# One maximum shared by two heads in pairs 3 to 10 of an attention and feed-forward kernel

## The chip, the cores and the metric

The kernel runs on one core of a Trainium2 chip. The metric is the device time of one launch in microseconds (us). Before the change it is 1376.97 us, the median of three runs (1376.26 to 1377.02).

## What is computed

Attention over 8 batches, 12 heads, 448 tokens and a head size of 64, with normalised q and k, and then a feed-forward layer over the 3584 tokens (768 wide, 2048 inside). Cut to what matters:

```
q_n, k_n = rmsnorm(q, g_q), rmsnorm(k, g_k)
scores = scale * (q_n @ k_n^T)
scores = scores - max(scores)            # per query
attn = exp(scores);  attn = attn / (sum(attn) + 1e-9)
x = (attn @ v), heads side by side       # 3584 x 768
r = relu(x @ w_in);  out = (s * r * r + b) @ w_out
```

The inputs are float32, and q, k, v and both gains come eight times as large as usual, so that scores are far apart. The kernel keeps the products exact by splitting a number into a high part in the format float32r, which TensorE multiplies in one pass, and the rest in a second one.

## The kernel before

Heads go in pairs: 48 pairs p = 0 to 47, six for each batch. A pair has eight slots, and slot 8p + 4j + kc holds one score tile `st` of head j: 128 keys against all 448 queries. One loop over slots writes every engine's instructions, and each engine runs its own in that order; PE is TensorE, DVE VectorE, ACT ScalarE, POOL GpSimd, and SP issues all DMA transfers, each once the semaphores of what it reads have come. What goes into a slot is set by `at(slot, function, ...)` and, for the maxima, by the table `scores`.

For a pair whose first slot is s0 = 8p, the steps near the change are, for p = 3 to 10:

- `load_rows` brings rows of k and q, `norm_rows` normalises them, `turn` transposes them on TensorE into `tk`, and `split_turned` (p under 8) or `split_both` and `split_lows` (from 8 on) write `ka` and `qa`. `ka` holds k's high part in rows 0 to 63 and its low part in rows 64 to 127; `qa` holds q's high part twice. For the second head this is at slots s0-9 and s0-8.
- `score` multiplies high and low k with every fourth query's high part, 112 queries by 448 keys, into the PSUM tile `sh`, and `maximum` takes the largest per query on DVE into a column of `nmx`. There are eight of them in a pair, c = 0 to 3 for the first head and 4 to 7 for the second, one to a slot, ten slots ahead of the slot with the same number: c = 3 in slot s0-7, c = 4 in s0-6, c = 7 in s0-3.
- `shift` moves the four columns of a head with a DMA into a row of `qb` (L431, `qb<-nmx`), in slots s0-6 and s0-2; `double_kb` copies k's high part into `kb` (`kb<-ka`).
- `score_t` (L496 and L499) writes the score tile with the shift already subtracted, ACT takes the exponential, and `weigh` multiplies it with v (`av`).
- `take`, `gather`, `invert` and `divide` bring the sums of the exponentials through DRAM: row to column (`zt`), inverse on DVE, out to `z_d`, and back as `zb`, spread over 64 rows for each head, in slot s0+16 of a pair. Slot s0-8 of one pair is slot s0+16 of the pair three before, and SP's order there is that of the pairs, the older first (pair 5's `zb` is entered by a loop of its own and stands behind).

From pair 12 (`TURNED`) on, a pair takes seven maxima: six over 128 of the first 384 queries, each third one, and one over the last 64 queries of both heads at once, which multiplies `qz` (the two heads' queries on the diagonal, zeros elsewhere) with `kh`, the high parts of both heads' k one above the other. There ACT writes both (`split_kq`, `both_k`). From pair 7 on, TensorE also runs the first feed-forward product of the batch before (`ph`), and DVE, ACT and POOL turn the weights, which come as 64-bit words (`w64i`), into two float32r parts (`wai`, `wih`, `wil`) in the first twelve pairs.

Of the kernel before, what the change touches and what calls it, by code (L numbers as in the profile page):

```python
# [9 lines left out]
F32 = mybir.dt.float32  # L10
F32R = mybir.dt.float32r
I32 = mybir.dt.int32
AF = mybir.ActivationFunctionType
ALU = mybir.AluOpType
# [11 lines left out]
AHEAD = 10  # L26
# [11 lines left out]
SHIFTED = {0: -9, 1: -8, 2: -7, 3: -6, 4: -4, 5: -3, 6: -2, 7: -1, 8: 1, 9: 1, 10: 2, 11: 2, 12: 4, 13: 4, 14: 5, 15: 5, 16: 8, 17: 8, 18: 9, 19: 10}  # L38
# [9 lines left out]
TURNED = 12  # L48

APART = 8  # L50

PLAIN = 11

THIRD = (11, 14, 17)

# [6 lines left out]
def attention_then_relu2_ffn(  # L62
# [30 lines left out]
    V, S, G, T = nc.vector, nc.scalar, nc.gpsimd, nc.tensor  # L93

    NPAIR, P, _, SEQ = kq.shape
# [4 lines left out]
    D = P // 2  # L100
    NP = NPAIR // B
    H = 2 * NP
    TILES = 2 * SEQ // P
    NV = PLAIN
    NQ = 4
    QC = SEQ // NQ
    WHOLE = SEQ // P * P
# [3 lines left out]
    NKC = 4  # L111
# [6 lines left out]
    W = 8  # L118
# [22 lines left out]
    def psum(name):  # L141

        bank = free.pop(0)
        return ps.tile([P, 512], F32, tag=bank, name=name), bank
# [85 lines left out]
    with tc.tile_pool(name="apool", bufs=1) as ap:  # L230
        khs = {}
        raws, kqs, invs, vrs, nmxs, shs, tks = ({} for _ in range(7))
# [102 lines left out]
        vs = [None, None]  # L335
# [10 lines left out]
        def split_v(p):  # L346
            n = p % 2
            if vs[n] is None:
                vs[n] = ap.tile([P, NKC, 2, 3, D], F32R, tag=f"vs{n}", name=f"vs{n}")
                for m in range(2):  # L350
                    G.memset(vs[n][:, :, m, 1].bitcast(F32), 1.0 - m)
            vr, to = vrs.pop(p), vs[n]
            S.copy(to[:, :, 0, 0:3:2], vr)
            G.tensor_tensor(to[:, :, 1, 0:3:2], vr, to[:, :, 0, 0:3:2].bitcast(F32), ALU.subtract)  # L354

        def norm(p):

# [38 lines left out]
        ka = [ap.tile([P, 2 * SEQ], F32R, name=f"ka{n}") for n in range(2)]  # L396
        qa = [ap.tile([P, 2 * SEQ], F32R, name=f"qa{n}") for n in range(2)]
        kb = [ap.tile([P, 2 * SEQ], F32R, name=f"kb{n}") for n in range(2)]
        qb = [ap.tile([P, 2 * SEQ], F32R, name=f"qb{n}") for n in range(2)]
        qz = ap.tile([P, P], F32R, name="qz")  # L400
        G.memset(qz.bitcast(F32), 0.0)
        for t in qb:
            G.memset(t[D:P].bitcast(F32), 0.0)
        vfs = [ap.tile([P, NKC, 3, D], F32, tag=f"vs{n}", name=f"vf{n}") for n in range(2)]
        for t in vfs:
            G.memset(t[:, :, 1], 1.0)
            G.memset(t[:REST, 3, 1], 0.0)
# [3 lines left out]
        def split_kq(p, j):  # L411

            t, n = kqs[p, j], p % 2
            a = slice(j * SEQ, (j + 1) * SEQ)
            S.copy(ka[n][:, a], t[:, 0])  # L415
            S.copy(qa[n][:, a], t[:, 1])
            half = slice(j * D, (j + 1) * D)
            S.copy(qz[half, half], t[half, 1, WHOLE:])
            yield
            G.tensor_tensor(ka[n][D:, a], t[D:, 0], ka[n][D:, a].bitcast(F32), ALU.subtract)  # L420
            G.tensor_tensor(qb[n][:D, a], t[:D, 1], qa[n][:D, a].bitcast(F32), ALU.subtract)  # L421

        def both_k(p):
            kqs.pop((p, 0))
# [5 lines left out]
        def move(to, of):  # L430
            nc.sync.dma_start(to.bitcast(F32), of.bitcast(F32))  # L431
# [5 lines left out]
        def score(i):  # L437

            p, c = divmod(i, W)
            j, c = divmod(c, NQ)  # L440
            sh, bank = psum(f"sh{i}")
            a = slice(j * SEQ, (j + 1) * SEQ)
            shs[i] = sh, bank
            if p >= TURNED:
                q, k = qz, khs.get(p)
                if i % W != 3:
                    q = qa[p % 2][:, a][:, :WHOLE].rearrange("k (p c) -> k c p", c=3)[:, c]
                    k = ka[p % 2][:, a]
                else:
                    khs.pop(p)  # L450
                T.matmul(sh[:, :SEQ], q, k, start=True, stop=True)  # L451
                return
            T.matmul(  # L453
                sh[:QC, :SEQ], qa[p % 2][:, a].rearrange("k (p c) -> k c p", c=NQ)[:, c],
                ka[p % 2][:, a], start=True, stop=True,
            )

        def maximum(i):
            p, c = divmod(i, W)
            if c == 0:  # L460
                nmxs[p] = bounds.tile([P, W], F32R, tag="nmx", bufs=2, name=f"nmx{p}")
            sh, bank = shs.pop(i)
            n = QC if p < TURNED else P
            V.tensor_reduce(  # L464
                out=nmxs[p][:n, c : c + 1], in_=sh[:n, :SEQ], op=ALU.max, axis=AX.X, negate=True
            )
            free.append(bank)

        def shift(p, part):

            to = qb[p % 2][D : D + 1, part * SEQ : (part + 1) * SEQ]
            if p < TURNED:
                of = nmxs[p][:QC, part * NQ : (part + 1) * NQ]
                move(to.rearrange("o (p c) -> o p c", c=NQ), of)
            else:
                of = nmxs[p][:, 4 * part : 4 * part + 3]
                move(to[:, :WHOLE].rearrange("o (p c) -> o p c", c=3), of)
                of = nmxs[p][part * D : (part + 1) * D, 3:4]
                move(to[:, WHOLE:].rearrange("o (p c) -> o p c", c=1), of)
            if part:  # L480
                nmxs.pop(p)
# [59 lines left out]
        def weigh(i):  # L541


            p, j, kc, rows = chunk(i)
            if kc == 0:
                avs[p, j] = psum(f"av{p}_{j}")
            av = avs[p, j][0]
            moved = movers.pop(i)
            if p < NV:
                of = vrs[p].rearrange("p c u d -> p c (u d)")  # L550
                todo = [(of[:, kc, j * D : j * D + P], moved[0])]
            else:
                of = vs[p % 2].rearrange("p c m u d -> p c m (u d)")
                hi, lo = (of[:, kc, m, j * D : j * D + P] for m in range(2))
                todo = [(hi, moved[0]), (lo, moved[0])] + [(hi, a) for a in moved[1:]]
            for m, (x, a) in enumerate(todo):
                T.matmul(  # L557
                    av[:, :SEQ], x, a,
                    start=kc == 0 and m == 0, stop=kc == 3 and m == len(todo) - 1,
                )  # L560
# [141 lines left out]
        def at(s_, f, *a):  # L702
            jobs[s_].append((f, a))
# [4 lines left out]
        for p in range(NPAIR):  # L708
            s0 = W * p
            if p >= TURNED:  # L710
                late_by = 2 if p == TURNED else 0
                at(s0 - 32 + 2 * late_by, load, p)
                after_x = 1 if p % NP == NP - 1 else 0
                at(s0 - 28 + late_by + after_x, norm, p)
                at(s0 - 24 + late_by + after_x, keep, p)
            for j in range(2):
                s1 = s0 + 4 * j
                steps = SOONER.get((p, j), (s1 - 20, s1 - 14, s1 - 13, s1 - 10, s1 - 6))
                if p >= TURNED:
                    apart = 1 if p % NP == 3 and j == 0 else 0  # L720
                    at(s1 - 19 + apart, load_kq, p, j)
                    at(s1 - 19 + (apart if j == 0 else 1), spread, p, j)
                    at(s1 - 15 + apart, scale, p, j)
                    at(s1 - 15 + apart, multiply_q if apart else scale_q, p, j)
                    at(s1 - 13, split_kq, p, j)
                    if j:
                        at(s0 - 8, both_k, p)
                else:
                    at(max(s1 - 28, FIRST), load_rows, p, j)
                    if s1 == 0:  # L730
                        at(FIRST, gains)
                    at(steps[0], norm_rows, p, j)
                    at(steps[1], turn, p, j)
                    if p < APART:
                        at(steps[2], split_turned, p, j)
                    else:
                        at(steps[2], split_both, p, j)
                        at(steps[2] + 1, split_lows, p, j)
                at(steps[3], double_kb, p, j)
                at(steps[4], shift, p, j)  # L740
                at(s1 + 6, take, p, j)
                at(s1 + 7, gather, p, j)
            at(s0 - (9 if p >= NV else 5), load_v, p)
            if p >= NV:
                at(s0 - 3, split_v, p)
            at(s0 + 13, invert, p)
            for step in (1, 2, 3):
                if p % NP < NP - 1:
                    at(s0 + 12 + 2 * step, divide, p, step)
# [21 lines left out]

        scores = {}
        for i in range(NSLOT):
            if i // W >= TURNED and i % W == W - 1:
                continue
            scores.setdefault(SHIFTED.get(i, i - AHEAD), []).append(i)

        def within(i):
            return 0 <= i < NSLOT
# [2 lines left out]
        with tc.manual_schedule(engines=ORDERED):  # L782
            begun = []
            for s_ in range(FIRST, NSLOT + START + NCC):
# [34 lines left out]
                b, m = divmod(s_ + 1 - START, W * NP)  # L819
# [271 lines left out]
```

## Time and profile before

| | before |
|---|---|
| median of three runs | 1376.97 us |
| span of the profiled execution, first to last instruction | 1375.6 us |
| busy PE, DVE, ACT, POOL | 99%, 77%, 68%, 44% of the span |
| maxima on DVE (L464) | 348 instructions, 212.8 us |
| score matmuls for them (L451, L453) | 252 + 96 by the maxima's shapes |

The span runs from the first to the last instruction of one profiled execution, and the median of the timed runs is 1.4 us above it. A share is busy time over the whole span. PE's records overlap, because matmuls are pipelined and their ends are modelled, so a matmul's own duration is longer than the distance from one start to the next. In the rows below SPq is SP's DMA queue, and its durations are those of the issue, not of the transfer.

### The profile page before, as it was taken

The numbers are of one execution on the slowest core, as the hardware profiler recorded it, in microseconds if no ns is written. First come the engines' busy times: TensorE is split into PE (matmuls) and PEld (weight loads), VectorE is DVE, ScalarE is ACT, GpSimd is POOL, SyncE is SP. The second block draws the span as 40 slices with busy tenths as digits, with TensorE's granted clock in tenths as the row PEclk, the third lists the DMA queues.
The fourth block names the chain that finished last, engine by engine and source line by source line (L and its number), as shares of the span: only waits on it lengthen the run. The fifth ranks groups of instructions, "written<-read, shape, count | busy, mean of one in ns | idle before, by whom it ended". The sixth has DMA issues, their size and how long they took to land.

```text
span 1375.6 us, 21578 instructions
## 1 busy us (share of the span) xinstructions
PE 1363.6 (99%) x6970; PEld 1255.6 (91%) x6970; DVE 1057.3 (77%) x1572; ACT 937.2 (68%) x1727; POOL 603.1 (44%) x486
## 2 busy tenths in 40 slices
PE   8999999999999999999999999999999999999998
PEld 7767789999999999999999999999999999999998
DVE  7999997897888798688788878526766676666763
ACT  6886778888888888888888887636544434344431
POOL 6875787766667666676667665100000000000000
PEclk9999999999999999999999999999999999999999
DMA  4555676787788788778778867356543332343330
GB/s 133 150 145 169 181 232 197 230 249 214 223 235 239 222 243 232 221 222 250 229 220 240 236 204 211 104 197 222 186 119 118 88 91 90 95 121 112 85 90 35
DMA packets 262800, 243.39 MB, mean 177 GB/s; under 512 B 85280, under 2 KB 244000, under 8 KB 262688
## 3 DMA queue, kind: packets, MB, share of 16 engines
q1 hardware_dynamic: 262688, 242.03, 60.0%
q8 instruction: 55, 0.90, 0.3%
q14 instruction: 57, 0.47, 0.1%
HBM read 177.21 MB, written 53.38 MB: 168 GB/s over the span
## 4 chain that ended last, share of the span: by engine, by line
PE 92%; DVE 4%; ACT 2%; DMA 1%; issue 1%; SPq 0%; POOL 0%; DVEq 0%; POOLq 0%; ACTq 0%
PE ph L198 32%; PE p L936 30%; PE av L557 15%; PE st L496 5%; PE st L499 5%; PE sh L451 4%; PE sh L453 1%; DVE nmx L464 1%; PE tk L282 1%; DVE wai L154 1%; DVE ssq L260 0%; DVE wai L152 0%; DVE wai L157 0%; DMA zb<-z_d 0%; ACT e L511 0%
## 5 line engine op out<-in xcount | busy, mean ns | idle before, releaser
L198 PE MATMUL ph<-x,wih 128*128 128x448 f32 x1536 | 488.3, 365 | 0.0
L198 PEld LDWEIGHTS ph<-x,wih 128*128 128x128 f32 x1536 | 289.0, 188 | 28.7 <-issue 6.1
L198 PE MATMUL ph<-x,wil 128*128 128x448 f32 x768 | 293.3, 382 | 0.0
L515 ACT ACTIVATE st<-st 128x448 f32<-128x448 f32 (+1 forms) x296 | 155.9, 527 | 104.1 <-PE st L499 102.7
L464 DVE TENSOR_REDUCE nmx<-sh 128x1 fp32r<-128x448 f32 (+1 forms) x348 | 212.8, 616 | 12.0 <-PE sh L451 6.3
L538 DVE TENSOR_TENSOR low<-st,ah 128x448 fp32r<-128x448 f32 x222 | 136.7, 616 | 47.2 <-ACT ah L523 42.5
L557 PE MATMUL av<-ah,vs 128*128 128x448 f32 x592 | 168.7, 366 | 0.0
L496 PE MATMUL st<-qa,ka 128*128 128x448 f32 (+1 forms) x384 | 159.1, 414 | 2.3 <-DVE nmx L464 2.2
L198 PEld LDWEIGHTS ph<-x,wil 128*128 128x128 f32 x768 | 144.3, 188 | 17.0 <-issue 6.2
L523 ACT CAST ah<-st 128x448 fp32r<-128x448 f32 (+1 forms) x296 | 156.9, 530 | 2.0
L499 PE MATMUL st<-qb,kb 128*128 128x448 f32 (+1 forms) x384 | 140.3, 365 | 0.0
L557 PEld LDWEIGHTS av<-ah,vs 128*128 128x128 f32 x592 | 111.2, 188 | 8.6
L921 ACT CAST hi<-a 128x1024 fp32r<-128x1024 f32 x54 | 56.8, 1053 | 91.0 <-PE p L936 74.0
L420 POOL TENSOR_TENSOR ka<-kq,ka 64x448 fp32r<-64x448 f32 x72 | 86.2, 1198 | 56.3 <-ACT ka L415 53.0
L603 POOL TENSOR_TENSOR u<-uz,zb 128x448 f32<-128x448 f32 x48 | 59.9, 1247 | 95.9 <-DMA zb<-z_d 75.9
L421 POOL TENSOR_TENSOR qb<-kq,qa 64x448 fp32r<-64x448 f32 x72 | 95.3, 1323 | 5.4
L369 POOL TENSOR_TENSOR ri<-ri,mhalf 128x14 f32<-128x14 f32 x36 | 93.6, 2601 | 3.0
L922 DVE TENSOR_TENSOR lo<-s,hi 128x1024 fp32r<-128x1024 f32 x41 | 50.1, 1222 | 52.1 <-ACT hi L921 52.1
L218 ACT ACTIVATE r<-ph 128x448 f32<-128x448 f32 x128 | 69.7, 545 | 27.6 <-PE ph L198 15.8
L354 POOL TENSOR_TENSOR vs<-vr,vs 128x512 fp32r<-128x512 f32 x37 | 49.4, 1336 | 86.0 <-DMA w64o<-in_dram 31.4
L496 PEld LDWEIGHTS st<-qa,ka 128*128 128x128 f32 (+1 forms) x384 | 68.2, 178 | 20.2 <-DVE nmx L464 6.1
L385 POOL TENSOR_TENSOR kq<-kq,rb 128x448 f32<-128x448 f32 x72 | 86.5, 1202 | 0.0
(253 smaller groups left out, 3256.4 us busy)
## 6 DMA issues: line engine op xcount, KB each, us to landing
kq<-in_dram SPq DMA_DIRECT2D x72, 448.0 KB, 5.1
rb<-i_d SPq DMA_DIRECT2D x72, 448.0 KB, 4.8
r_d<-r SPq DMA_DIRECT2D x128, 224.0 KB, 3.7
a<-r_d SPq DMA_DIRECT2D x48, 512.0 KB, 4.9
raw<-in_dram SPq DMA_DIRECT2D x36, 448.0 KB, 5.0
w64i<-in_dram SPq DMA_DIRECT2D x24, 512.0 KB, 4.5
w64o<-in_dram SPq DMA_DIRECT2D x48, 256.0 KB, 4.1
kb<-ka SPq DMA_DIRECT2D x96, 112.0 KB, 2.8
```

Of the source, the lines that this page charges most:

```text
L198: T.matmul(ph[:, :SEQ], w[:, cc, f0 : f0 + P], xs[b, cc][:, part, :], start=cc == 0 and m == 0, stop=cc == NCC - 1 and m == 2,)
L369: G.tensor_tensor(ri, ri, mhalf[:, :n], ALU.pow)
L385: G.tensor_tensor(t[:, 0], t[:, 0], rb[:, 0], ALU.mult)
L421: G.tensor_tensor(qb[n][:D, a], t[:D, 1], qa[n][:D, a].bitcast(F32), ALU.subtract)
L464: V.tensor_reduce(out=nmxs[p][:n, c : c + 1], in_=sh[:n, :SEQ], op=ALU.max, axis=AX.X, negate=True)
L496: T.matmul(st[:rows, :SEQ], ka[n][:, keys], qa[n][:, q], start=True, stop=False)
L499: T.matmul(st[:rows, :SEQ], kb[n][:, keys], qb[n][:, q], start=False, stop=True,)
L515: S.activation(st[:rows, :SEQ], st[:rows, :SEQ], AF.Exp)
L523: S.copy(ah[:rows], sts[i][0][:rows, :SEQ])
L538: V.tensor_tensor(al, st[:rows, :SEQ], ah[:rows].bitcast(F32), ALU.subtract)
L557: T.matmul(av[:, :SEQ], x, a, start=kc == 0 and m == 0, stop=kc == 3 and m == len(todo) - 1,)
L936: T.matmul(po, a[:, f], w[:, f], start=f == 0 and m == 0, stop=f == NH - 1 and m == 2,)
```

## The change

Pairs 3 to 10 take seven maxima too. `score` and `maximum` go the way of the later pairs for them. `last_queries` lets ACT copy the last 64 queries of each head into `qz`, and `join_k` lets two DMAs move the high parts of both heads' k from `ka` into `kh`; both are entered in slot s0-8. The shared maximum, c = 3, goes from slot s0-7 to s0-6, where c = 4 is, and c = 7 falls away. The shift of the first head goes one slot later, to s0-5, and each shift takes two DMAs instead of one. `kh` lies in the room of v's low part, which these pairs don't use yet; for that the tile `vs` is cut into two. Lines of the changed kernel are up to 21 higher: L467 and L469 are the score matmuls, L447 the moves, L598 `zt`, L614 `zb`.

```
+SHARED = frozenset(range(3, PLAIN))
...
-                vs[n] = ap.tile([P, NKC, 2, 3, D], F32R, tag=f"vs{n}", name=f"vs{n}")
+                vs[n] = [ap.tile([P, NKC, 3, D], F32R, tag=f"v{x}{n}", name=f"v{x}{n}") for x in "hl"]
...
+        def shared(p):
+            return p >= TURNED or p in SHARED
+
+        def last_queries(p):
+            for j in range(2):
+                half = slice(j * D, (j + 1) * D)
+                S.copy(qz[half, half], qa[p % 2][half, j * SEQ + WHOLE : (j + 1) * SEQ].bitcast(F32))
+
+        def join_k(p):
+            kh = khs[p] = ap.tile([P, SEQ], F32R, tag=f"vl{p % 2}", name=f"kh{p}")
+            for j in range(2):
+                a = slice(j * SEQ, (j + 1) * SEQ)
+                move(kh[j * D : (j + 1) * D], ka[p % 2][:D, a])
...
-            if p >= TURNED:
+            if shared(p):
                 q, k = qz, khs.get(p)
...
-            n = QC if p < TURNED else P
+            n = P if shared(p) else QC
...
-            if p < TURNED:
+            if not shared(p):
                 of = nmxs[p][:QC, part * NQ : (part + 1) * NQ]
...
-                at(steps[4], shift, p, j)
+                at(steps[4] + (p in SHARED and j == 0), shift, p, j)
+                if p in SHARED and j:
+                    at(steps[3] - 2, last_queries, p)
+                    at(steps[3] - 2, join_k, p)
...
-            if i // W >= TURNED and i % W == W - 1:
+            if shared(i // W) and i % W == W - 1:
                 continue
-            scores.setdefault(SHIFTED.get(i, i - AHEAD), []).append(i)
+            sooner = AHEAD - (i // W in SHARED and i % W == NQ - 1)
+            scores.setdefault(SHIFTED.get(i, i - sooner), []).append(i)
```

On SP the first place is pair 3's slots 16 to 19. Before, with `zb_700` of pair 0, row loads of pairs 5 and 6, and the moves of pair 3 (`kb_194`, `qb_196`):

```order
L597 DMA zb_700<-z_d_87 64x448 x2
L245 DMA rows_1_705<-in_dram 112x512
L431 DMA qb_196<-nmx_672 1x112x4
L431 DMA kb_194<-ka_190 64x448
L581 DMA zt_656<-zr_735 64x1x7
```

and now:

```order
L614 DMA zb_700<-z_d_87 64x448 x2
L447 DMA kh_705<-ka_190 64x448 x2
L247 DMA rows_1_710<-in_dram 112x512
L447 DMA kb_194<-ka_190 64x448
L598 DMA zt_656<-zr_737 64x1x7
L447 DMA qb_196<-nmx_672 1x128x3
L447 DMA qb_196<-nmx_672 1x64x1
```

The two joining moves stand behind `zb`, and the shift, now in two pieces, stands behind the doubling of `kb` and the gathering of `zt`.

On PE the place is pair 3's slots 16 to 18, `sh` being the maxima's score tiles (c = 2, 3 and 4 of pair 3 before) and `tk` the transposes of pair 4:

```order
L453 MATMUL sh_707<-ka_190,qa_192 112x448
L557 MATMUL av_1_675<-e_648,vf_202 128x448
L496 MATMUL st_712<-qa_191,ka_189 128x448
L499 MATMUL st_712<-qb_195,kb_193 128x448
L453 MATMUL sh_719<-ka_190,qa_192 112x448
L557 MATMUL av_1_675<-e_680,vf_202 128x448
L496 MATMUL st_724<-qa_191,ka_189 128x448
L499 MATMUL st_724<-qb_195,kb_193 128x448
L282 MATMUL tk_0_0_740<-ident,rows_0_460 64x112 x4
L282 MATMUL tk_0_1_745<-ident,rows_0_460 64x112 x4
L453 MATMUL sh_750<-ka_190,qa_192 112x448
```

and now:

```order
L467 MATMUL sh_712<-ka_190,qa_192 128x448
L574 MATMUL av_1_675<-e_648,vf_202 128x448
L512 MATMUL st_717<-qa_191,ka_189 128x448
L515 MATMUL st_717<-qb_195,kb_193 128x448
L574 MATMUL av_1_675<-e_680,vf_202 128x448
L512 MATMUL st_726<-qa_191,ka_189 128x448
L515 MATMUL st_726<-qb_195,kb_193 128x448
L284 MATMUL tk_0_0_741<-ident,rows_0_460 64x112 x4
L284 MATMUL tk_0_1_746<-ident,rows_0_460 64x112 x4
L467 MATMUL sh_751<-kh_705,qz 128x448
L467 MATMUL sh_753<-ka_190,qa_192 128x448
```

The slot in the middle has no score matmul any more, and the one that reads `kh` and `qz` stands right ahead of c = 4, behind the transposes.

## Rows read from the trace of the kernel before

**Rows 1.** Three stretches: length, busy us (instructions) of each engine, granted clock, DMA.

```profile
core 0: us, PE busy (x) PEld busy (x) DVE busy (x) ACT busy (x) POOL busy (x), PEclk, DMA share, GB/s
...
28.00:68.00 40.00, 39.87 (x175) 28.73 (x174) 36.97 (x70) 35.07 (x70) 27.71 (x24) 1.00 0.55 150
68.00:139.00 71.00, 67.25 (x286) 49.28 (x284) 68.37 (x111) 56.17 (x109) 46.84 (x38) 1.00 0.56 157
139.00:175.00 36.00, 35.74 (x159) 29.26 (x160) 34.01 (x53) 27.50 (x51) 28.75 (x21) 1.00 0.63 180
```

**Rows 2.** PE's waits from 68 to 139 us: total us, times, longest us.

```profile
PE st L496 <- DVE nmx L464: 1.6, 2, 0.8
PE sh L453 <- DVE nmx L464: 1.1, 1, 1.1
PE sh L453 <- DVE ka L310: 0.6, 1, 0.6
```

**Rows 3.** Instructions by line and form: busy us, mean ns of one, idle before.

```profile
L464 DVE TENSOR_REDUCE nmx<-sh 112x1 fp32r<-112x448 f32 x96 | 57.5, 614 | 2.1 <-PE sh L453 1.7
...
L453 PE MATMUL sh<-ka,qa 128*112 128x448 f32 x96 | 38.5, 418 | 3.5 <-DVE ka L294 1.2 <-DVE nmx L464 1.1 <-DVE ka L310 0.6
```

**Rows 4.** Line 418, ACT's copy of last queries: ns min/median/max, first and last start.

```profile
L418 ACT CAST qz<-kq x72: 238/242/247, 184.0 to 857.7; 64x64 fp32r<-64x64 f32 x72
```

**Rows 5.** PE in order of time, at pairs 3, 4, 7, 9: start, us.

```profile
42.36 0.36 PE L453 MATMUL sh<-ka,qa 128*112 128x448 f32 x1
...
43.71 0.36 PE L453 MATMUL sh<-ka,qa 128*112 128x448 f32 x1
43.91 0.91 PE L557 MATMUL av<-e,vf 128*128 128x448 f32 x2
...
45.76 0.54 PE L453 MATMUL sh<-ka,qa 128*112 128x448 f32 x1
...
58.39 0.54 PE L453 MATMUL sh<-ka,qa 128*112 128x448 f32 x1
...
98.29 0.54 PE L453 MATMUL sh<-ka,qa 128*112 128x448 f32 x1
...
136.55 0.54 PE L453 MATMUL sh<-ka,qa 128*112 128x448 f32 x1
```

**Rows 6.** SP's issues in order of time, at pairs 3, 4, 7, 9.

```profile
42.68 0.54 SPq L162 DMA_DIRECT2D w64i<-in_dram  x1
43.31 1.10 SPq L597 DMA_DIRECT2D zb<-z_d  x2
44.51 0.52 SPq L245 DMA_DIRECT2D rows<-in_dram  x1
...
57.56 0.53 SPq L245 DMA_DIRECT2D rows<-in_dram  x1
...
97.22 1.09 SPq L597 DMA_DIRECT2D zb<-z_d  x2
...
132.41 1.10 SPq L597 DMA_DIRECT2D zb<-z_d  x2
```

**Rows 7.** DMA issues, at pairs 3, 7, 9, and all kb: KB, us to landing.

```profile
w64i<-in_dram SPq DMA_DIRECT2D x1, 512.0 KB, 4.4
zb<-z_d SPq DMA_DIRECT2D x2, 112.0 KB, 4.2
...
zb<-z_d SPq DMA_DIRECT2D x2, 112.0 KB, 4.1
...
zb<-z_d SPq DMA_DIRECT2D x2, 112.0 KB, 3.9
...
kb<-ka SPq DMA_DIRECT2D x96, 112.0 KB, 2.8
```

**Rows 8.** DVE in order of time, at pairs 3 and 7.

```profile
46.32 1.14 DVE L464 TENSOR_REDUCE nmx<-sh 112x1 fp32r<-112x448 f32 x2
...
101.02 1.14 DVE L464 TENSOR_REDUCE nmx<-sh 112x1 fp32r<-112x448 f32 x2
```

More of the change, by code (lines that the diff above doesn't have):

```diff
@@ L348, in split_v @@
             if vs[n] is None:
-                vs[n] = ap.tile([P, NKC, 2, 3, D], F32R, tag=f"vs{n}", name=f"vs{n}")
+                vs[n] = [ap.tile([P, NKC, 3, D], F32R, tag=f"v{x}{n}", name=f"v{x}{n}") for x in "hl"]
                 for m in range(2):
[L351 to L354, printed above, removed]
+                    G.memset(vs[n][m][:, :, 1].bitcast(F32), 1.0 - m)
+            vr, (hi, lo) = vrs.pop(p), (x[:, :, 0:3:2] for x in vs[n])
+            S.copy(hi, vr)
+            G.tensor_tensor(lo, vr, hi.bitcast(F32), ALU.subtract)
         def norm(p):
@@ L403, in attention_then_relu2_ffn @@
             G.memset(t[D:P].bitcast(F32), 0.0)
-        vfs = [ap.tile([P, NKC, 3, D], F32, tag=f"vs{n}", name=f"vf{n}") for n in range(2)]
+        vfs = [ap.tile([P, NKC, 3, D], F32, tag=f"vh{n}", name=f"vf{n}") for n in range(2)]
         for t in vfs:
@@ L552, in weigh @@
             else:
-                of = vs[p % 2].rearrange("p c m u d -> p c m (u d)")
-                hi, lo = (of[:, kc, m, j * D : j * D + P] for m in range(2))
+                hi, lo = (
+                    x.rearrange("p c u d -> p c (u d)")[:, kc, j * D : j * D + P] for x in vs[p % 2]
+                )
                 todo = [(hi, moved[0]), (lo, moved[0])] + [(hi, a) for a in moved[1:]]
```

## The prediction

> **What bounds the kernel now.** I read the stretches of the run first, then who waits for whom, then the two or three microseconds around the place that the change touches. Names: pair p is counted from 0, so the change acts on p = 3 to 10; each pair has eight slots, one score tile per slot; c is the number of a maximum within its pair (0 to 3 for the first head, 4 to 7 for the second).
>
> By stretch [rows 1]: pairs 3 and 4 have their scores and maxima between 28 and 68 us, pairs 5 to 9 between 68 and 139, pair 10 after that. In the first stretch PE is busy 39.87 of 40 us: TensorE sets the pace, at 1.35 us a slot (two score matmuls in a row start at 42.36 and 43.71 [rows 5]), and DVE (36.97) follows. In the second both are nearly full, DVE 68.37 and PE 67.25 of 71: neither has room there, and PE's own waits in it, 1.6 + 1.1 + 0.6 = 3.3 us [rows 2], are all for DVE. After 139 us PE is again the limit (35.74 of 36). So a microsecond in which PE stands still costs a microsecond before 68 us and after 139 us, and part of one between.
>
> **What goes.** Eight score matmuls and eight maxima (c = 7 of each pair). A matmul of 448 columns has 0.42 us of recorded duration [rows 3], but what it takes from PE is the distance to the next start: 43.71 to 43.91, 0.20 us [rows 5]. Eight are worth 1.6 us where PE sets the pace. A maximum is 0.61 us [rows 3], and two back to back take 1.14, so 0.57 each [rows 8]: eight are worth 4.6 us where DVE does. By stretch: p = 3, 4 and 10 at 0.20, p = 5 to 9 at 0.57, together 3.5 us at best. The other maxima take 128 queries instead of 112 of each key row; the maximum's time doesn't depend on it.
>
> **What comes on ACT.** Two 64x64 copies a pair, 0.24 us each by the same copy in later pairs [rows 4]: 16 x 0.24 = 3.9 us on ACT, which is busy 35 of 40 us and 56 of 71 [rows 1]. They stand two slots ahead of their reader. I cost them at nothing, since ACT has that room; without the cover they would cost at most 3.9 us, and they cannot gain.
>
> **What comes on SP and in the DMA queue.** Per pair two moves that join k_hi (112 KB each, like the doubling of kb) and two more moves for the shift, since each part now goes in two pieces: four issues of about 0.55 us, 2.3 us of SP a pair. The shift of the first half goes a slot later, five slots before its use, which is 6.8 us at 1.35 us a slot; the slowest landing among the rows is 4.4 us [rows 7], so I cost it at nothing, with a loss of some 0.5 us a pair as the other end.
>
> **The new wait.** The maximum c = 3 is now one for both heads. It reads kh, the joined k_hi, and so PE waits for two transfers. Before, it read only what ACT and DVE had written. In PE's order its matmul moves from slot s0-7 into s0-6, ahead of c = 4. The question is when PE gets there and when kh lands. I work it out for p = 3, on the rows of the kernel before.
>
> PE: the matmul of c = 4 starts at 45.76 [rows 5]. The shared one stands ahead of it, and one matmul of the slot before is gone, so PE is there at 45.56.
>
> SP: the joining moves stand behind the two zb loads and ahead of the row load. SP issues the zb loads at 43.31 (1.10 us for both) and the row load at 44.51 [rows 6]; so the two kh moves are issued at 44.5 and 45.1. Their source is ready by then, but ahead of them in the queue lie a 512 KB weight piece (issued 42.68, landed 4.4 us later) and the zb loads, which took 4.2 us because of it [rows 6, 7]. The second zb load lands at 43.8 + 4.2 = 48.0, and two more transfers of the same size follow at the same distance as the two zb loads, 0.5 us each: kh is there at 49.0. PE stands 49.0 - 45.56 = 3.4 us. Behind the waiting matmul in PE's queue lie c = 4, the av product and the next score tiles, and behind their outputs ACT's exponentials; DVE, in order too, would reach the shared maximum at 46.3 [rows 8] and waits as well.
>
> The same reading for the others. With a weight piece ahead: p = 7, zb issued 97.22, the second at 97.7, + 4.1 + 1.0 = 102.8, against 98.29 - 0.2 = 98.1: 4.7 us [rows 5 to 7]; p = 5 has this pattern, and I put it between, at 3.6. Without a piece ahead (p = 4, 6): the second move is issued 0.55 us after the place of the row load, 57.56 + 0.55 = 58.1, and lands 2.8 us later, the median of the kb moves [rows 6, 7]: 60.9 against 58.39 - 0.2 = 58.2, so 2.7; I take 2.6 for both. In pairs 8 to 10 a slot is longer, since TensorE does matmuls of the next part in it: p = 9, second zb 132.9 + 3.9 + 1.0 = 137.8 against 136.55 - 0.2 = 136.35, so 1.4; I take 1.5 for the three. Together PE would stand 3.4 + 2.6 + 3.6 + 2.6 + 4.7 + 3 x 1.5 = 21.4 us.
>
> [...] In the rows a zb load behind a weight piece takes 4.1 to 4.2 us, while kb moves of that size have a median of 2.8 [rows 7], so transfers here wait for what was issued ahead. [...]
>
> **What of it is paid.** Before 68 us: p = 3 and 4 in full, 3.4 + 2.6 = 6.0, less 0.4 for their two matmuls: +5.6. After 139 us: p = 10, 1.5 - 0.2 = +1.3. Between, p = 5 to 9 stand 3.6 + 2.6 + 4.7 + 3.0 = 13.9 us by PE's count. From above: less the 3.3 us that PE waited for DVE anyway and 5 x 0.2: +9.6. From below, DVE's count: at p = 7 DVE comes to the maximum at 101.02 [rows 8] and finds it ready at 102.8 + 0.4 (the matmul) = 103.2, 2.2 us of waiting; I take 1.5 for p = 5 and 6, which lie less late, and 0 for 8 and 9; 5.2 - 5 x 0.57 = +2.3. I take +5.0, a little under the middle, because each stall lets DVE catch up with PE, and with it the z chain that the zb loads hang on. Sum: 5.6 + 5.0 + 1.3 = 11.9 us.
>
> The rows come from one execution with a span of 1375.6 us; the median of the timed runs is 1.4 above that. I add the change to the median: 1377.0 + 11.9 = 1388.9.
>
> **Rivals.**
> *The joined k_hi is there in time.* Then only the savings count: 3.5 us less, 1373.5. For it: both sources are long written when the moves are issued. Against it: at p = 3 the second move is issued at 45.1, and kb's median would still put it at 47.9, 2.3 us after PE; to be hidden it would have to be issued 3.4 us earlier than where it stands behind zb. Chance 0.06.
> *The stalls die out.* After the first one or two, SP, DVE and the transfers have run ahead of PE by the length of the stall, and the later kh are there when PE comes. Then p = 3 costs 3.4, p = 4 about 2, and the rest gains or loses 1 or 2: +2 to +5, about 1380. For it: the z gather stands ahead of the shared maximum on ACT and SP. Against it: the z inversion stands behind it on DVE, and zb follows from that. Chance 0.17.
> *All stalls are paid.* The 2.3 us more of SP's time a pair puts the weight pieces off too, and DVE's count follows PE's: 21.4 - 1.6 = +19.8, 1397. Chance 0.10.
> *TensorE's clock falls in the stalls.* [...] No row here shows a fall, so the chance is 0.08. [...]
> *The sums cancel.* Stalls of some 4 us against savings of as much: within 0.2% (2.8 us, about what a measurement of this kernel can tell from no change). Chance 0.04.
>
> **How the numbers follow.** The forecast, between +6 and +17, has 0.55. Faster by over 0.2%: the first rival, 0.06. Within 0.2%: 0.04 and a small part of the second rival, together 0.07. Slower: 0.87. The range goes from 1379.5 (most of the second rival) to 1399 (all stalls paid); what is left out are the first rival, the clock and the edge of the second.
>
> **What would show it.** In the profile after: PE waits of 1 to 5 us ahead of the matmul that reads kh and qz, once in each of the eight pairs, with a DMA of kh as the releaser; kh landing 3 to 5 us after its issue, behind zb; DVE waiting for that matmul in pairs 3 and 4; 340 maxima instead of 348; PE's clock at 1.00. It would be wrong if the waits were there at p = 3 and gone from p = 5 on, or if kh were issued ahead of zb.

## The result, and the profile after

The changed kernel takes 1391.37 us (median of four runs, 1388.78 to 1392.67) against 1376.99 us before in the same comparison (1376.26 to 1377.41). The ratio is 1.0098, 95% interval 1.0085 to 1.0110: 14.4 us slower. The forecast was 1388.9 us, range 1379.5 to 1399.0. Two executions of one later version, with its maximum one slot later, were disturbed as a whole (5049 us, and 1487 us at a lower clock) and are compared with nothing.

The page of the profiled execution, first its span and then busy us, share and instructions of each engine:

```profile
span 1390.6 us, 21609 instructions
...
PE 1365.4 (98%) x6962; PEld 1256.7 (90%) x6962; DVE 1056.8 (76%) x1564; ACT 940.4 (68%) x1743; POOL 594.6 (43%) x486
```

PE and DVE have eight instructions less each and ACT sixteen more, as the change says; the span is 15.0 us longer. So the added work is small, and the time has to be looked for in waits and in the clock. By stretch, answering to [rows 1]; the third row is the rest of the attention part:

```profile
core 0: us, PE busy (x) PEld busy (x) DVE busy (x) ACT busy (x) POOL busy (x), PEclk, DMA share, GB/s
28.00:68.00 40.00, 34.09 (x144) 24.01 (x142) 31.35 (x57) 29.70 (x62) 20.24 (x19) 0.96 0.52 143
68.00:139.00 71.00, 62.73 (x263) 45.78 (x261) 58.68 (x99) 54.89 (x112) 42.36 (x37) 0.95 0.53 150
...
250.00:870.00 620.00, 619.57 (x3047) 567.45 (x3046) 521.76 (x845) 524.75 (x1093) 416.99 (x325) 1.00 0.78 229
```

PE is busy 34.09 of the 40 us where it was busy 39.87, and both stretches of the change have a granted clock under 1.00. From 250 to 870 us PE is busy without a break, as it was before (619.57 and 619.77 us): what was lost is lost before that and isn't given back.

The waits of PE that the kernel before doesn't have (total us, times, longest); where [rows 2] had waits for DVE from 68 to 139 us, none is left:

```profile
PE sh L467 <- DMA kh<-ka: 12.8, 5, 4.5
PE sh L467 <- ACT wih L152: 3.2, 1, 3.2
PE sh L467 <- DVE wai L156: 1.7, 1, 1.7
```

All seven stand ahead of the matmul that reads kh and qz. Two (pairs 6 and 7) are put down to ACT and DVE; but in each of the seven PE starts 0.14 us after the second half of kh has landed (kh at 97.19 and PE at 97.33 us in pair 6, 112.49 and 112.63 in pair 7), so these two are for kh as well. In order of time at pair 3, PE, answering to [rows 5]:

```profile
44.82 0.83 PE L284 MATMUL tk<-ident,rows 112*64 112x112 f32 x7
50.19 0.44 PE L467 MATMUL sh<-kh,qz 128*128 128x448 f32 x1 [4.54 <-DMA kh<-ka]
50.47 0.43 PE L467 MATMUL sh<-ka,qa 128*128 128x448 f32 x1
50.70 1.70 PE L574 MATMUL av<-e,vf 128*128 128x448 f32 x2
```

SP's issues there, answering to [rows 6]:

```profile
43.02 0.33 SPq L164 DMA_DIRECT2D w64i<-in_dram  x1
43.45 1.10 SPq L614 DMA_DIRECT2D zb<-z_d  x2
44.60 1.23 SPq L447 DMA_DIRECT2D kh<-ka  x2
45.94 0.52 SPq L247 DMA_DIRECT2D rows<-in_dram  x1
```

and the time from issue to landing of these, answering to [rows 7]:

```profile
w64i<-in_dram SPq DMA_DIRECT2D x1, 512.0 KB, 4.5
zb<-z_d SPq DMA_DIRECT2D x2, 112.0 KB, 5.6
kh<-ka SPq DMA_DIRECT2D x2, 112.0 KB, 5.0
```

PE comes at 45.65 (50.19 less the wait of 4.54), kh is issued at 44.60 and 45.23 and lands 5.0 us later, behind a weight piece and two zb loads. DVE, which reached the place at 46.32 in [rows 8], stood too:

```profile
45.94 0.67 DVE L262 TENSOR_REDUCE ssq<-sq 112x8 f32<-112x512 f32 x1
50.67 1.16 DVE L480 TENSOR_REDUCE nmx<-sh 128x1 fp32r<-128x448 f32 x2 [4.07 <-PE sh L467]
```

By pair: the wait from PE's records, the start of the pair's own first score tile `st` (slot 8p, some ten slots behind its maxima) in both kernels, and what was lost between the first tile of the pair before and this one:

| pair | wait forecast | wait | its first tile starts, before / after | lost up to it |
|---|---|---|---|---|
| 3 | 3.4 | 4.5 | 54.2 / 60.2 | 6.1 |
| 4 | 2.6 | 1.3 | 67.2 / 74.0 | 0.9 |
| 5 | 3.6 | 3.4 | 81.7 / 91.4 | 2.9 |
| 6 | 2.6 | 1.7 | 94.5 / 105.7 | 1.4 |
| 7 | 4.7 | 3.2 | 108.7 / 121.9 | 2.1 |
| 8 | 1.5 | 0 | 130.3 / 142.3 | -1.2 |
| 9 | 1.5 | 2.5 | 152.7 / 166.3 | 1.5 |
| 10 | 1.5 | 1.0 | 174.3 / 188.9 | 1.0 |

Pair 8 has no wait for kh and is 1.2 us shorter than before. Most of that is a wait of PE for DVE that the kernel before had there and that is gone:

```profile
127.58 0.47 PE L496 MATMUL st<-qa,ka 128*128 128x448 f32 x1 [0.84 <-DVE nmx L464]
```

In pair 8 kh stands ahead of zb, since pair 5's zb loads are entered by a loop of their own. SP's issues at pair 8, and PE's shared matmul, which waits for nothing:

```profile
122.39 0.51 SPq L598 DMA_DIRECT2D zt<-uz  x1
122.96 1.24 SPq L447 DMA_DIRECT2D kh<-ka  x2
124.30 0.53 SPq L247 DMA_DIRECT2D rows<-in_dram  x1
124.94 1.10 SPq L614 DMA_DIRECT2D zb<-z_d  x2
```

```profile
127.12 0.45 PE L467 MATMUL sh<-kh,qz 128*128 128x448 f32 x1
```

And the clock did fall, at the three longest waits: 0.4 us behind the end of the wait in pair 3, and 0.2 and 0.6 us before the end of those in pairs 5 and 7. In three of these stretches the granted clock, the third number from the right, is 0.50, where every stretch of [rows 1] has 1.00; in the second row it is back at 1.00.

```profile
50.62:54.03 3.41, 3.41 (x8) 2.05 (x7) 2.66 (x5) 0.79 (x2) 0.48 (x1) 0.50 0.18 39
54.04:60.00 5.96, 5.96 (x28) 4.39 (x27) 4.70 (x11) 4.58 (x10) 1.89 (x3) 1.00 0.53 149
81.35:84.75 3.40, 3.19 (x7) 2.23 (x8) 2.41 (x4) 0.00 (x0) 2.90 (x3) 0.50 0.09 13
112.07:115.47 3.40, 2.84 (x6) 1.93 (x7) 2.09 (x3) 0.46 (x1) 3.24 (x4) 0.50 0.29 82
```

PE's rows in the first stretch and behind its end show what this does to the matmuls:

```profile
52.56 0.58 PE L515 MATMUL st<-qb,kb 128*128 128x448 f32 x1
52.94 0.58 PE L467 MATMUL sh<-ka,qa 128*128 128x448 f32 x1
53.31 1.28 PE L574 MATMUL av<-e,vf 128*128 128x448 f32 x2
...
54.63 0.36 PE L515 MATMUL st<-qb,kb 128*128 128x448 f32 x1
54.83 0.37 PE L467 MATMUL sh<-ka,qa 128*128 128x448 f32 x1
```

From one start to the next are 0.38 and 0.37 us at the clock of 0.50, and 0.20 at 1.00. So I count 3.4 us at 0.50 as 1.7 us of work. By this estimate the fall in pair 3 costs 1.7 us; those in pairs 5 and 7, part of which lies inside the wait, cost 1.6 and 1.4. That explains pair 3: 4.5 of wait + 1.7 of clock - 0.2 saved = 6.0, against 6.1 lost. The fall isn't peculiar to this one execution: all four timed runs have a mean granted clock of 0.995 or 0.996, where the kernel before has 0.999 to 1.000 in every run of the experiments.

### The profile page after: what moved, and what is told of

Same layout as the page of the kernel before. It is cut to its first block, busy times and chain, and to the rows that moved or that the text cites. A ratio compares the mean times of both kernels' runs of the same rounds, so it can differ in the third digit from the quotient of the medians.

```text
span 1390.6 us, 21609 instructions
## 1 busy us (share of the span) xinstructions
PE 1365.4 (98%) x6962; PEld 1256.7 (90%) x6962; DVE 1056.8 (76%) x1564; ACT 940.4 (68%) x1743; POOL 594.6 (43%) x486
## 4 chain that ended last, share of the span: by engine, by line
PE 92%; DVE 2%; ACT 2%; DMA 1%; issue 1%; POOL 1%; SPq 0%; ACTq 0%; DVEq 0%; POOLq 0%
PE ph L200 32%; PE p L957 29%; PE av L574 15%; PE st L512 5%; PE st L515 5%; PE sh L467 4%; DMA kh<-ka 1%; DVE nmx L480 1%; PE tk L284 0%; DVE wai L156 0%; PE warmth L331 0%; PE sh L469 0%; ACT e L527 0%; ACT qa L294 0%; ACT x L627 0%
## 5 line engine op out<-in xcount | busy, mean ns | idle before, releaser
L480 DVE TENSOR_REDUCE nmx<-sh 128x1 fp32r<-128x448 f32 (+1 forms) x340 | 207.6, 615 | 26.7 <-PE sh L467 20.9
L574 PE MATMUL av<-ah,vh 128*128 128x448 f32 x296 | 108.5, 367 | 0.0
L574 PE MATMUL av<-ah,vl 128*128 128x448 f32 x296 | 108.2, 366 | 0.0
L467 PE MATMUL sh<-ka,qa 128*128 128x448 f32 x264 | 98.1, 372 | 0.0
L356 POOL TENSOR_TENSOR vl<-vr,vh 128x512 fp32r<-128x512 f32 x37 | 49.4, 1336 | 85.9 <-issue 37.2
L515 PEld LDWEIGHTS st<-qb,kb 128*128 128x128 f32 (+1 forms) x384 | 68.7, 179 | 19.2 <-issue 10.6
```

The costliest lines, as they stand in the source:

```text
L480: V.tensor_reduce(out=nmxs[p][:n, c : c + 1], in_=sh[:n, :SEQ], op=ALU.max, axis=AX.X, negate=True)
L515: T.matmul(st[:rows, :SEQ], kb[n][:, keys], qb[n][:, q], start=False, stop=True,)
L574: T.matmul(av[:, :SEQ], x, a, start=kc == 0 and m == 0, stop=kc == 3 and m == len(todo) - 1,)
```

## The experiments

Theory W: PE waits for kh, and kh lands late because of where its two moves stand in SP's order. Rival T: the four more issues a pair and their bytes put off SP's other transfers, and PE's wait is only where that shows. All diffs are against the changed kernel, the verdicts against the kernel before on the same chip.

**Moves one slot sooner.** They stand right behind the copies that write their source, ahead of the weight piece and zb.

```
-                    at(steps[3] - 2, join_k, p)
+                    at(steps[2], join_k, p)
```

> Both joining moves are entered one slot sooner, right behind the copy that writes their source and ahead of the weight piece and the zb loads in SP's order; nothing else changes. Theory W (PE waits for kh, which lands late because it stands behind a weight piece and the zb loads): kh lands near the time PE comes, the waits shrink from 17.6 us to 2 to 4, the clock no longer falls, and the time is 1375 to 1379 us. Rival T (the extra issues and bytes put off SP's other transfers, and PE's wait is only where that shows): as many moves as before, so 1386 to 1391 us.

Measured: 1377.83 us (1374.9 to 1380.77) against 1377.39, ratio 1.0005 (0.9996 to 1.0013). The loss is gone with as many transfers as before; T falls. SP's issues at pair 3 now, the landing, and PE at the same place:

```profile
42.00 0.59 SPq L598 DMA_DIRECT2D zt<-uz  x1
42.64 1.23 SPq L447 DMA_DIRECT2D kh<-ka  x2
43.97 0.54 SPq L164 DMA_DIRECT2D w64i<-in_dram  x1
44.60 1.96 SPq L614 DMA_DIRECT2D zb<-z_d  x2
```

```profile
kh<-ka SPq DMA_DIRECT2D x2, 112.0 KB, 2.3
```

```profile
45.90 0.45 PE L467 MATMUL sh<-kh,qz 128*128 128x448 f32 x1
```

Issued 2 us sooner, the same move lands in 2.3 us instead of 5.0 and PE doesn't wait. Four waits of 0.6 to 1.4 us are left, at pairs 4, 6, 7 and 8, and each ends 0.14 us after kh has landed; with 4.7 us they are more than the 2 to 4 expected. The clock stays at 1.00. In this profile, of the fastest of its runs, the kernel is 2.7 us ahead of before from pair 12 on; in the median nothing of that is seen.

**ACT joins.** Two copies by ACT write kh, the first line below from PSUM right behind the split of the second head, the last one added from `ka`, in `last_queries`.

```
+                kh = khs[p] = ap.tile([P, SEQ], F32R, tag=f"vl{p % 2}", name=f"kh{p}")
+                S.copy(kh[D:], k)
...
+            S.copy(khs[p][:D], ka[p % 2][:D, :SEQ].bitcast(F32))
...
-                move(kh[j * D : (j + 1) * D], ka[p % 2][:D, a])
```

> ACT writes kh with two copies of 64x448 (about 0.55 us each) instead of the two transfers; all else as changed. W: no wait for a transfer at the shared maximum, ACT has 1.1 us more a pair: 1374 to 1379 us. T: two of the four extra issues a pair are gone, so about half of the loss stays, 1382 to 1386 us.

Measured: 1378.48 us, ratio 1.0013 (1.0004 to 1.0022). The loss is gone here too, and the two copies took 0.51 and 0.55 us (medians of eight), but the savings don't show: PE now waits for ACT's exponential (1.3 + 0.8 us), for k's low part from DVE (1.3 us), which itself waited up to 1.6 us for ACT's new copy, and for rows from POOL (0.7 + 0.4 us). ACT is busier between 28 and 139 us:

```profile
28.00:68.00 40.00, 39.17 (x170) 27.18 (x169) 35.40 (x65) 36.86 (x76) 24.89 (x23) 1.00 0.54 150
68.00:139.00 71.00, 68.26 (x288) 48.92 (x287) 65.71 (x109) 63.60 (x131) 45.38 (x39) 1.00 0.56 157
```

ACT has 63.60 of 71 us where [rows 1] had 56.17. That ACT's load is what takes the savings is likely, and not shown by a run of its own.

**Idle moves.** As the last, with two transfers a pair from the old place into room that nothing reads.

```
+            for j in range(2):
+                n = NKC * 3 * D - SEQ
+                move(t[j * D : (j + 1) * D], ka[p % 2][:D, j * SEQ : j * SEQ + n])
```

> As with ACT joining kh, but two transfers a pair (64x320 instead of 64x448) are issued from the old place into room that nothing reads. W: no one waits for them, so within 3 us of the kernel in which ACT joins. T: the transfers load SP and the queue as before, so 1386 to 1391 us.

Measured: 1378.81 us, ratio 1.0008 (0.9999 to 1.0016), within 0.4 us of the last one. Two transfers a pair that no one waits for cost nothing that can be measured. (They are 64x320, not 64x448.)

**Maximum one slot later.** The shared maximum is at s0-5 and the first head's shift at s0-4; the moves stay.

```
-            sooner = AHEAD - (i // W in SHARED and i % W == NQ - 1)
+            sooner = AHEAD - 2 * (i // W in SHARED and i % W == NQ - 1)
-                at(steps[4] + (p in SHARED and j == 0), shift, p, j)
+                at(steps[4] + 2 * (p in SHARED and j == 0), shift, p, j)
```

> The shared maximum and the shift of the first head go one more slot later (s0-5 and s0-4); the moves stay where they are. W: each wait shrinks by a slot, 1.4 us: 4.5, 1.3, 3.4, 1.7, 3.2, 2.5, 1.1 become about 3.1, 0, 2, 0.3, 1.8, 0, 0; with one or two falls of the clock 1381 to 1386 us. T: nothing about the transfers changes, 1390 to 1392 us.

Measured: 1381.18 us, ratio 1.0025 (1.0014 to 1.0036), runs from 1376.3 to 1385.6: most of the loss goes when PE comes later, as W has it, at the lower end of the expected range. The same kernel once more, for its waits:

> The kernel with the shared maximum one slot later once more, for its profile. W: waits for kh of about 3, 0, 2, 0.3, 1.8, 0, 0 us in pairs 3 to 10, at most one fall of the clock.

Measured: 1487.43 us at a granted clock of 0.85 throughout, so at full clock the single waits of this kernel stay unseen.

**Idle matmuls in the waits.** Twelve matmuls on a spare PSUM bank ahead of the shared one, in pairs 3, 5 and 7 (they are float32, and the trace has 24 records for the twelve; a float32r score matmul has one, as the 44 on kh and qz in 44 pairs of the changed kernel).

```
+            if c == NQ - 1 and p in (3, 5, 7) and j == 0:
+                warm_up(12)
```

> The changed kernel with twelve idle matmuls of 128 columns (0.2 to 0.25 us each, about 2.6 us) ahead of the shared maximum of pairs 3, 5 and 7, the three after whose waits the granted clock fell to half for 3.4 us each. They lie inside waits of 3.2 to 4.5 us, so they delay nothing. If the falls cost what half a clock takes from PE's work (C1), 3 x 1.7 = 5.1 us come back: about 1386. If DVE or the transfers limit there anyway (C2), the falls are free and the time stays at 1391 within 1 us.

Measured: 1393.12 us, ratio 1.0116 (1.0102 to 1.0130). Neither expectation was met as written: the time is 16.2 us above before, where the changed kernel was 14.4 above. At pair 3 the clock's price shows: the idle matmuls keep PE busy for 2.86 us, and the granted clock stays at 1.00.

```profile
45.63 2.86 PE L331 MATMUL warmth<-ident 128*128 128x128 f32 x24
49.77 0.44 PE L469 MATMUL sh<-kh,qz 128*128 128x448 f32 x1 [1.29 <-DMA kh<-ka]
```

and by stretch, the first right behind that wait, the others at the end of pair 4's and 1.0 us behind pair 6's:

```profile
50.60:54.00 3.40, 3.40 (x14) 2.37 (x13) 3.33 (x7) 2.29 (x5) 0.48 (x1) 1.00 0.21 45
64.30:67.70 3.40, 3.31 (x7) 2.35 (x8) 2.56 (x3) 0.03 (x1) 3.32 (x3) 0.50 0.78 224
98.50:101.80 3.30, 3.30 (x7) 1.93 (x7) 3.30 (x4) 1.79 (x4) 2.38 (x3) 0.50 0.71 195
```

Pair 3 loses 3.9 us instead of 6.1. Counted from pair 2's first tile, kh landed 0.6 us sooner, and the other 1.6 fit the 1.7 worked out for the clock. But what pairs 3, 5 and 7 give back, pairs 4 and 6 lose (3.3 and 4.1 us instead of 0.9 and 1.4): PE waits 2.1 and 2.9 us there instead of 1.3 and 1.7, and now the clock falls there. In pair 4 PE comes 2.1 us sooner than in the changed kernel and kh lands only 1.2 us sooner: kh stands behind zb, and zb follows the sums of older pairs over DVE and other transfers.

**Both: moves sooner and maximum later.**

> The joining moves one slot sooner and the shared maximum one slot later, both at once. With the moves sooner four waits of 0.6 to 1.4 us (4.7 in all) were left. W: a slot of 1.4 us takes all of them away and the savings of 3.5 us show: 1373 to 1376. The rival (the shift of the first head now comes too late for its score tile, four slots instead of five): a new wait of PE for the transfer into qb, 1377 to 1380.

Measured: 1379.78 us, ratio 1.0020 (1.0011 to 1.0029). Waits for kh are gone, but neither the savings nor the rival's wait for qb came. A wait that nobody had forecast is there instead: c = 0 of the next pair reads ka's low part, which DVE writes behind two maxima in a row, a step of the weights of 1.96 us and one more maximum. PE, and then DVE, ahead of pair 7's first tile:

```profile
108.94 0.74 PE L467 MATMUL sh<-ka,qa 128*128 128x448 f32 x1 [2.22 <-DVE ka L312]
```

```profile
104.69 1.15 DVE L480 TENSOR_REDUCE nmx<-sh 128x1 fp32r<-128x448 f32 x2
105.75 1.96 DVE L156 SCALAR_TENSOR_TENSOR wai<-w64i,wai 128x512 int32<-128x512 int32 x1
107.63 0.61 DVE L480 TENSOR_REDUCE nmx<-sh 128x1 fp32r<-128x448 f32 x1
108.27 0.62 DVE L312 TENSOR_TENSOR ka<-tk,ka 64x448 fp32r<-64x448 f32 x1
```

At the end of this wait the clock falls too:

```profile
108.81:112.22 3.41, 3.28 (x7) 2.31 (x8) 2.96 (x7) 1.68 (x4) 1.12 (x2) 0.50 0.90 268
```

That doesn't explain the median, though: the four of the eleven runs with a mean clock of 1.000 took 1379.3 to 1381.6 us, the others 1377.3 to 1380.3. What the rest of the 2.9 us is stays open.

**The same from pair 5 on.**

```
-SHARED = frozenset(range(3, PLAIN))
+SHARED = frozenset(range(5, PLAIN))
```

> As the kernel with moves sooner and maximum later, but pairs 3 and 4 keep eight maxima (pairs 5 to 10 share). There PE sets the pace, and a shared maximum saves only 0.2 us each: 0.4 us slower than the kernel with all eight pairs if no wait was left in these two, up to 1 us faster if one was; 1374 to 1376.

Measured: 1377.83 us against 1376.91, ratio 1.0011 (1.0002 to 1.0020): 2.0 us better than the last, above the expected range. The same wait for DVE, 2.0 us, is there, and a fall of the clock behind it (107.44 to 110.85 us).

**The first head's half four slots sooner, the second's one.**

```
-                    at(steps[3] - 2, join_k, p)
+                if p in SHARED:
+                    at(steps[2] + 1 - j, join_k, p, j)      # join_k moves one half
```

> The move of the first head's half is entered four slots sooner than in the change (s0-12), the second head's one slot sooner (s0-9); the shared maximum stays at s0-6. Only one move is left between the copy that writes its source and PE. W: the waits that were left with both moves one slot sooner (1.4, 1.4, 0.6, 1.3) shrink by one issue, 0.6 us each: 2 to 3 us of waiting in all, 1374 to 1378 us. T: 1386 to 1391 us, as many transfers as before.

Measured: 1378.69 us, ratio 1.0009 (1.0000 to 1.0017): as with both moves one slot sooner. The waits for kh are 0.9 to 1.7 us, four of them, 4.6 us in all where 2 to 3 were expected, so one issue less didn't show as such.

**Moves one slot later.**

```
-                    at(steps[3] - 2, join_k, p)
+                    at(steps[3] - 1, join_k, p)
```

> The joining moves one slot later (s0-7), behind the row load of 224 KB as well; the shared maximum stays at s0-6. W: kh lands 1 to 2 us later in each pair, seven to eight waits instead of seven, 28 to 34 us in all, with more falls of the clock: 1400 to 1412 us. T: the same transfers in nearly the same order, 1390 to 1394 us.

Measured: 1404.31 us, ratio 1.0191 (1.0176 to 1.0207), inside W's range. The waits sum to 23.3 us, fewer than the 28 to 34 expected, 4.8 at the longest; seven of the eight pairs have one:

```profile
PE sh L467 <- DMA kh<-ka: 23.3, 7, 4.8
```

and the granted clock is at 0.50 for 27.3 us, where the changed kernel has 10.2. Two of the six stretches are of 6.8 us, the first at pair 3:

```profile
48.36:55.19 6.83, 4.39 (x10) 2.98 (x10) 2.84 (x6) 0.97 (x3) 2.88 (x3) 0.50 0.31 69
```

One slot sooner, as changed, one slot later: 1377.8, 1391.4, 1404.3 us, for two moves of the same bytes.

## Why the prediction was right

The step that carried it, kh landing behind zb and PE standing before it, is shown: it is in the trace in seven pairs, in four of them (3, 5, 7 and 10) with a weight piece ahead as well; it goes with the moves' place (both directions) and with the transfers themselves, and extra transfers that nothing waits for cost nothing that was measured (1378.81 us with the idle moves, 1378.48 without). Some of the signs named in advance did not come: the clock was not at 1.00, pair 8 had no wait, kh's landing took 2.2 to 5.3 us and not 3 to 5, and DVE waited for the shared matmul in pair 3 (4.1 us) but hardly in pair 4 (0.2 us). In pair 8 kh was issued ahead of zb, which the prediction had called a sign of being wrong; it holds for that pair.

That the sum of 11.9 came within 2.5 us of the 14.4 is in part luck: the waits were 3.7 us shorter than forecast, and the clock, which the sum put at nothing, added some 4.7. By its terms:

*Waits.* 17.7 us were measured in place of 21.4. Pair 3, worked out at 3.4, was 4.5; the zb loads took 5.6 us there and not 4.2. With the idle matmuls zb took 3.8 us at the same place and kh still landed only 0.4 us sooner, so what holds kh up behind zb isn't settled. Pairs 4 and 6 were 1.3 and 1.7 instead of 2.6: after a stall DVE, and with it zb, is further ahead of PE. SP's move of the inverses to DRAM (`z_d<-zt`), which waits for DVE, was issued 0.5 us ahead of pair 3's first tile before (53.67 us) and 2.0 us ahead of it now (58.20). That is the relief that the second rival rested on; it took about half of these two waits and didn't end them. Pair 8 was an error of reading: the order of zb and kh is turned round there, as SP's order had shown, and I took the pair with 9 and 10.

*What is paid.* Forecast 5.6 for pairs 3 and 4, 5.0 for 5 to 9 and 1.3 for 10; measured 7.0, 6.8 and 1.0.

*The clock* was a rival of its own, with a chance of 0.08, since none of its rows shows a fall; three falls came, worth 1.7, 1.6 and 1.4 us by the estimate above. They belong to the forecast's waits, and without them the forecast's sum would have been too high.

*What goes.* PE's eight matmuls were put at 0.20 us each, 1.6 in all. That a maximum takes as long over 128 queries as over 112 is so in the kernel before: 616 ns (252 instructions of L464) and 614 ns (96). From pair 2's first tile to pair 11's, PE's rows before, as changed, and with the moves one slot sooner are:

```profile
41.59:194.81 153.22, 149.20 (x644) 113.72 (x643) 147.03 (x235) 120.14 (x231) 112.01 (x88) 1.00 0.62 177
41.45:209.46 168.01, 150.36 (x636) 114.19 (x635) 144.87 (x227) 123.67 (x247) 104.74 (x88) 0.97 0.59 172
41.55:192.19 150.64, 145.70 (x636) 111.39 (x635) 140.15 (x227) 123.97 (x247) 105.01 (x88) 1.00 0.67 192
```

With the moves sooner and the clock at 1.00 PE is busy 145.7 us, 3.5 less than before and not 1.6; as changed, 150.36 less the 4.7 of the clock is the same 145.7. With that the account closes: 17.7 of waits and 4.7 of clock, less 3.5 of PE's busy time and the 4.0 that PE stood before, make 14.9, against 14.8 lost in this stretch. Why eight matmuls take 3.5 us of busy time with them is open; with ACT joining kh, PE is busy 149.3 us in this stretch, so that nothing of it is seen there.

In the traces before and as changed none of SP's transfers (1202 and 1234) lands before one that was issued ahead of it. kh took 2.3 us when issued ahead of the weight piece and zb, and 5.0 behind them, as the prediction read it from the rows.

*The rival "in time"* priced the savings at 3.5 us. In no version were they seen in a median: 1377.8 to 1379.8 us for the six whose waits for kh are short or gone, none faster than before. In the one profile with 2.7 us gained, 4.7 us of waits were left where before there were 4.0, which fits savings of 3.5; but it is one execution, the fastest of eleven. In the others waits for kh, ACT, DVE or POOL of about a microsecond take their place; one profile for each version can't show how these change from run to run. Why these six scatter by 3 to 6 us between runs, and the kernel before by 3, stays open; the mean clocks of the runs don't go with it.

## What to carry to other kernels

When a step moves from an engine to the DMA queue, count what SP issues ahead of it and how large that is, not what one such transfer takes alone. Here a transfer of 2.3 us became one of 5.0 by standing behind 512 KB and two loads, and one slot sooner or later in SP's order was worth 13 us either way. And where the bounding engine waits for a chain that doesn't follow it at the same pace, as PE for kh here, speeding it up can lengthen the wait: in pairs 4 and 6 it was 2.1 and 2.9 us with the idle matmuls, and 1.3 and 1.7 without.

## What the hardware showed that I had not expected

At waits of 3.2 to 4.5 us TensorE's granted clock went from 1.00 to 0.50 for 3.4 us (for 6.8 twice, with the moves one slot later); a fall that lies behind the wait costs about 1.7 us by the estimate above, and the idle matmuls at pair 3 gave 1.6 back. The length of the wait alone doesn't decide it: no fall came at pair 9's 2.5 us in the changed kernel, and one came at 2.1 us with the idle matmuls and at 2.2 and 2.0 us in two other versions. Where TensorE is the bound, as at pair 3, such a stall cost 1.7 us more than its own 4.5, over a third; at the shorter waits of pairs 5 and 7 the same estimate gives nearly half.
